# The weighing loops of an attention kernel turned: key tile outside, the four heads inside

## The chip, the cores and the metric

The kernel runs on one core of one Trainium2 chip. The metric is the device time of one execution in microseconds (us). A core has a matrix engine (TensorE, PE in the profile, its weight loads PEld), three engines for elementwise work (VectorE, DVE; ScalarE, ACT; GpSimd, POOL) and a queue engine (SyncE, SP) that here issues transfers. Each engine works its own instructions in order, and they meet through semaphores. PE takes a stationary operand (128 rows by up to 128 columns, put in by a weight load) and streams a moving operand through it; the products are added up in PSUM, a memory of 8 banks, each of 512 fp32 columns on 128 partitions. A matmul with the first-flag (`start=True`) overwrites what stands in its columns; one without it adds to them, or, where nothing was written in the bank since the last first-flag, writes them.

## The reference

Attention with grouped heads, then a gated block with a spatial mix. There are 8 batches, 16 query heads, 4 key/value heads (each serves four query heads), 384 positions and 64 columns a head.

```
scores = q @ k.T / sqrt(64)
attn   = exp(scores - max) ; attn = attn / (sum(attn) + 1e-9)
x      = attn @ v                       # heads side by side: [8, 384, 1024]
h      = relu(x @ w_in)                 # 1024 -> 1024
u, v   = h[..., :512], h[..., 512:]
v_n    = (v - mean(v)) / sqrt(var(v) + 1e-6)
v_s    = w_spatial @ v_n + b_spatial    # mixes the 384 positions
out    = (u * v_s) @ w_out              # 512 -> 1024
```

## The kernel before

One batch has 384 positions, so three tiles of 128 queries (`qt`) and three of 128 keys (`kt`, `NT` = 3). The 16 query heads go as two halves (`j`) of two key/value heads (`hh`), each with its group of four query heads (`G` = 4, index `i`). A set (`s`) is one query tile and one `j`: there are 6 sets a batch and 48 in all. For each set and each `hh` and `kt` the kernel makes one score matmul (L278, 64 rows of contraction, 512 columns: the 128 queries of four heads) into a bank, and ACT takes the exponent of it (L290) into the fp16 tile `aT`, which is laid out `[128 keys, kt, hh, 4 x 128 queries]`. The maximum isn't subtracted.

`weigh(b, s, hh)` (L292) multiplies these by the values. It takes a fresh bank `av` and issues twelve matmuls (L298): for each of the four heads `i` and each key tile `kt`, the stationary operand is the 128x128 block of `aT`, and the moving operand is a slice of `v1` with 65 columns. The slice holds the 64 value columns and one column of ones, so that the 65th column of the result is the sum of the exponents. Slices of `v1` lie next to each other in the order `[key/value head, kt]`, each `VW = D + 2` = 66 fp16 columns long (L46, L173); 65 of the 66 are read. Head `i` owns columns 65i to 65i+64 of the bank. In the kernel before, the loop over heads is outside and the loop over key tiles inside, so that the three matmuls of one head follow each other and add to the same columns. The first of each three has the first-flag. Behind the twelve, DVE takes the reciprocal of the four sums (L311) and multiplies (L313) into the fp16 tile `x16`. `weigh` is called 96 times, which makes 1152 matmuls and 1152 weight loads.

The rest follows on `x16`. It is transposed to `xt`: for the first batch by PE (L330) and a copy, for the others by a DMA that SP issues (`x_send`, L334, called behind the second `weigh` of every second set). Then come x @ w_in (`pv` L353 for the v half, `pu` L412 for the u half, with the relu on ACT, L423), the normalisation on DVE, ACT and POOL, the spatial mix (`psp` L431), the gate on POOL (L448) and x @ w_out (`po` L469). Queries and keys are transposed by PE at the beginning (L224 and L238, against an identity matrix that is the moving operand) and by DMA later.

The order of the work is written out by the program. A loop of 21 single units (L717) starts it: in each, two score matmuls, two exponents, then `weigh` where a set has ended. The steady loop (L738) takes one set a turn: six score matmuls, three exponents, some matmuls of the second block ("pour", which draws on the generator `gated`), the second `weigh` of the set before, more pouring, three exponents, pouring, the first `weigh` of this set, pouring. How much is poured follows the planner's costs in ns (`spend`, L85), and `weigh` is entered there with 372 ns. The `bank` function (L77) takes the bank that the planner expects to be free first. The change touches none of these numbers, so that the planner's order of all other instructions stays.

The lines of `weigh`, and of what calls it:

Of the kernel before, what the change touches and what calls it, by code (L numbers as in the profile page):

```python
# [17 lines left out]
def kernel(  # L18
# [21 lines left out]
    NT = S // P  # L40
    NK = DM // P
    NM = DH // P
    G = HQ // HKV
# [33 lines left out]
    def bank(shape, dtype, name):  # L77
        i = min(range(8), key=done.__getitem__)
        t = ps.tile(shape, dtype, name=name, tag=f"bank{i}")
        clock[nc.tensor] = max(clock[nc.tensor], done[i])  # L80
        done[i] = 1e12 + clock[nc.tensor]
        taken[name] = i
        return t

    def spend(ns):  # L85
        clock[nc.tensor] += ns

    def reads(eng, ns, name=None):
        clock[eng] = max(clock[eng], clock[nc.tensor] + 200.0) + ns
        if name:  # L90
            done[taken.pop(name)] = clock[eng]
# [200 lines left out]
    def weigh(b, s, hh):  # L292
        qt, j = divmod(s, 2)
        aT = aTs[b, s]
        av = bank([P, 512], FP32, f"av_{b}_{s}_{hh}")
        for i in range(G):
            for kt in range(NT):
                nc.tensor.matmul(  # L298
                    av[:, i * (D + 1) : (i + 1) * (D + 1)],
                    aT[:, kt, hh, i * P : (i + 1) * P],  # L300
                    v1[b % 2][:, 2 * j + hh, kt, 0 : D + 1],
                    start=(kt == 0),
                    stop=(kt == NT - 1),
                )
        if s == 0 and hh == 0:
            x16s[b] = att.tile([P, NT, DM], FP16, name=f"x16_{b}", tag="x16")
        o = av[:, 0 : G * (D + 1)].rearrange("p (i d) -> p i d", i=G)
        spend(372)
        r = small.tile([P, G, 1], FP32, name=f"r_{b}_{s}_{hh}", tag="r")
        reads(dve, 600.0, f"av_{b}_{s}_{hh}")  # L310
        dve.reciprocal(r, o[:, :, D : D + 1])  # L311
        c = j * 512 + hh * 256
        dve.tensor_tensor(  # L313
            x16s[b][:, qt, c : c + 256].rearrange("p (i d) -> p i d", i=G),
            o[:, :, 0:D],
            r.to_broadcast([P, G, D]),
            ALU.mult,
        )
        measure()
# [54 lines left out]
    def measure():  # L374
        while unmeasured:
            b, st = unmeasured.pop()
            reads(dve, 800.0)
            stats = small.tile([P, 6], FP32, name=f"stats_{b}_{st}", tag="stats")
            dve.bn_stats(stats, v_r[b, st])  # L379
            dve.bn_aggr(mvs[b][:, st], stats)  # L380
# [336 lines left out]
    for u in range(ALONE):  # L717
        for pair in units(u, 1):
            exp(*pair)
        spare = 736  # L720
        for f, args in todo.pop(u, []):
            f(*args)
            spare -= 224 if f in (q_turn, x_turn, k_turn) else 0
        for b, s in ends.pop(u, []):
            halves.setdefault(u, []).append((b, s, 0))
            halves.setdefault(u + (0 if s == 0 else 1), []).append((b, s, 1))
        for h in halves.pop(u, []):
            weigh(*h)
            spare -= 372
            if h[2]:  # L730
                turn_x(*h[:2], u)
        owed = pour(u, min(owed, 0) + spare)
    for u in sorted(halves):
        for h in halves[u]:
            weigh(*h)
    owed = 0.0
    late = [(b, s, hh) for u in (ALONE, ALONE + 1) for b, s in ends.pop(u, []) for hh in range(2)]
    for n in range(ALONE, total, NT):  # L738
        share = STEP * (0.85 if n < 90 else 1.0)
        exps = units(n, NT)  # L740
        for pair in exps[:NT]:
            exp(*pair)
        owed = pour(n, owed + share * F[0])
        for h in late:
            weigh(*h)
            if h[2]:
                turn_x(*h[:2], n)
        owed = pour(n, owed + share * F[1])
        for u in range(n, n + NT):
            for f, args in todo.pop(u, []):  # L750
                f(*args)
        for pair in exps[NT:]:
            exp(*pair)
        owed = pour(n, owed + share * F[2])
        late = []
        for u in range(n, n + NT):
            for b, s in ends.pop(u + 2, []):
                weigh(b, s, 0)
                late.append((b, s, 1))
        owed = pour(n, owed + share * F[3])  # L760
# [36 lines left out]
```

## Time and profile before

| what | value |
|---|---|
| median of three runs | 241.03 us (239.21, 241.6, 241.03) |
| the profiled execution, its own time | 239.56 us |
| its span in the profile | 237.5 us |
| instructions | 5921 |
| granted clock of PE | 1.0 of full speed |
| PE busy / ACT busy / DVE busy / POOL busy | 97% / 71% / 60% / 42% |
| transfers | 47.47 MB, mean 200 GB/s |

The span is the time between the first and the last instruction that the profiler saw on the core; 2.06 us of the execution lie around it. Busy shares are of the span. Matmuls are pipelined: a matmul's duration in the profile runs from its start to the end of its last write, and the next one starts well before that. What a matmul costs in a dense stream is therefore read from the distance of two starts.

### The profile page before, as it was taken

The page shows a single profiled execution, that of the slowest core. Times are in us where ns is not written, and L with a number is a line of the kernel's source. Part 1 is how long each engine was busy: PE and PEld are TensorE (multiplying, and loading weights), DVE is VectorE, ACT ScalarE, POOL GpSimd, SP SyncE. Part 2 cuts the span into 40 slices and gives each one's busy share as a digit, 9 for nine tenths or more (in the row PEclk, how much of TensorE's full clock was granted, in tenths as well). Part 3 has the DMA queues.
Part 4 walks back from the last instruction along what each step waited for, and adds up shares of the span by engine and source line. Part 5 has one row for each costly group of instructions (what it writes and reads, how often), then busy time and mean ns, then how long its engine had stood idle before and what let it go on. Part 6 is the DMA issues. An engine that isn't in the chain of part 4 may idle for free.

```text
span 237.5 us, 5921 instructions
## 1 busy us (share of the span) xinstructions
PE 231.4 (97%) x2312; PEld 124.3 (52%) x2312; DVE 142.8 (60%) x379; ACT 169.2 (71%) x348; POOL 100.9 (42%) x145
## 2 busy tenths in 40 slices
PE   7999999999999999999999999999999999999993
PEld 6555565645554545555464445555465455545541
DVE  2668774676447674566645577366744667367362
ACT  2899979969897869977697776986597776401211
POOL 3769663651465432275045800565022500360550
PEclk9999999999999999999999999999999999999999
DMA  6999959998999999997996599829912543240147
GB/s 199 286 328 308 280 107 194 228 224 223 292 220 258 322 296 176 365 199 176 171 323 200 168 199 300 266 88 158 260 21 44 114 147 95 48 177 0 66 201 266
DMA packets 67467, 47.47 MB, mean 200 GB/s; under 512 B 48336, under 2 KB 60416, under 8 KB 67440
## 3 DMA queue, kind: packets, MB, share of 16 engines
q1 hardware_dynamic: 62512, 39.86, 66.6%
q0 software_dynamic: 3952, 6.42, 11.9%
q10 hardware_dynamic: 976, 0.82, 1.2%
q8 instruction: 18, 0.29, 0.5%
q14 instruction: 9, 0.07, 0.1%
HBM read 25.95 MB, written 12.58 MB: 162 GB/s over the span
## 4 chain that ended last, share of the span: by engine, by line
PE 93%; DVE 3%; DMA 2%; ACT 1%; issue 0%; ACTq 0%
PE pu L412 18%; PE pv L353 18%; PE po L469 17%; PE sc L278 16%; PE av L298 15%; PE psp L431 7%; DMA q<-in_q_dram 2%; PE qps L238 1%; DVE x L313 1%; ACT aT L290 1%; DVE qT L216 1%; PE xps L330 1%; DVE osb L216 1%; PE kps L224 0%; DVE r L311 0%
## 5 line engine op out<-in xcount | busy, mean ns | idle before, releaser
L290 ACT ACTIVATE aT<-sc 128x512 f16<-128x512 f32 x288 | 147.4, 625 | 32.0 <-PE sc L278 31.4
L298 PEld LDWEIGHTS <-aT 128*128 128x128 f16 x1152 | 47.7, 97 | 17.0 <-issue 1.6
L298 PE MATMUL av<-v,aT 128*128 128x65 f16 x1152 | 51.6, 193 | 0.1
L353 PE MATMUL pv<-w_in,xt 128*128 128x512 f16 x192 | 50.8, 379 | 0.1
L469 PE MATMUL po<-w_out,gT 128*128 128x512 f16 (+2 forms) x196 | 50.5, 375 | 0.0
L412 PE MATMUL pu<-xt,w_in 128*128 128x384 f16 x256 | 49.9, 326 | 0.0
L397 POOL TENSOR_SCALAR vn<-vr,rstd,nmr 128x512 f16<-128x512 f32 x23 | 17.6, 779 | 71.3 <-DVE nmr L392 49.8
L448 POOL TENSOR_TENSOR gT<-vs,uT 128x384 f16<-128x384 f32 x31 | 32.4, 1058 | 32.4 <-DVE r L311 17.1
L313 DVE TENSOR_TENSOR x<-av,r 128x256 f16<-128x256 f32 x96 | 40.7, 424 | 3.3
L278 PE MATMUL sc<-qT,kT 64*128 64x512 f16 x288 | 42.2, 380 | 0.4 <-DVE qT L216 0.2
L311 DVE RECIPROCAL r<-av 128x4 f32<-128x4 f32 x96 | 17.1, 178 | 41.2 <-PE av L298 41.0
L216 DVE COPY osb<-po 128x512 f32<-128x512 f32 (+1 forms) x39 | 26.5, 682 | 17.3 <-PE po L469 17.3
L412 PEld LDWEIGHTS <-w_in 128*128 128x128 f16 x256 | 22.1, 97 | 17.1 <-issue 5.5
L423 ACT ACTIVATE uT<-pu 128x384 f16<-128x384 f32 x32 | 15.8, 493 | 16.3 <-PE pu L412 16.1
L469 PEld LDWEIGHTS <-gT 128*128 128x128 f16 x196 | 17.4, 97 | 17.4 <-issue 2.8
L353 PEld LDWEIGHTS <-xt 128*128 128x128 f16 x192 | 15.8, 97 | 17.9 <-issue 5.7
L278 PEld LDWEIGHTS <-kT 64*128 64x128 f16 x288 | 10.9, 94 | 25.0 <-issue 13.8
L431 PE MATMUL psp<-wsT,vn 128*128 128x384 f16 x96 | 22.2, 326 | 0.0
L443 DVE TENSOR_TENSOR vs<-psp,bias_bc 128x384 f32<-128x384 f32 x32 | 17.5, 551 | 7.0 <-PE psp L431 6.9
L367 DVE TENSOR_SCALAR vr<-pv 128x512 f32<-128x512 f32 x24 | 16.4, 682 | 8.5 <-PE pv L353 8.4
L201 POOL CAST q<-q 128x768 f16<-128x768 f32 x22 | 17.6, 831 | 7.5 <-DMA q<-in_q_dram 5.5
L379 DVE BATCH_NORM_STATS2 stats<-vr 128x6 f32<-128x512 f32 x24 | 16.4, 685 | 0.1
(47 smaller groups left out, 98.6 us busy)
## 6 DMA issues: line engine op xcount, KB each, us to landing
out_dram<-osb SPq DMA_DIRECT2D x21, 512.0 KB, 2.8
q<-in_q_dram SPq DMA_DIRECT2D x10, 768.0 KB, 7.4
v_None<-in_v_dram SPq DMA_DIRECT2D x6, 384.0 KB, 4.6
w_in<-in_moe_w_in_dram POOLq DMA_DIRECT2D x4, 512.0 KB, 10.3
k_None<-in_k_dram SPq DMA_DIRECT2D x5, 384.0 KB, 3.9
q<-in_q_dram POOLq DMA_DIRECT2D x2, 768.0 KB, 8.9
out_dram<-osb SPq DMA_DIRECT2D x5, 256.0 KB, 2.3
w_out<-in_moe_w_out_dram POOLq DMA_DIRECT2D x2, 512.0 KB, 6.8
```

The lines of the kernel that those rows point to most:

```text
L201: eng.tensor_copy(t16[:, :, :, hh, :], src[:, hh])
L216: (act.copy if eng is act else dve.tensor_copy)(o, i)
L278: nc.tensor.matmul(sc, kTs[b][rows, j, kt * P : (kt + 1) * P], qTs[b, j][rows, qt].rearrange("p (r i c) -> p i r c", r=G, i=G), start=True ...
L290: act.activation(a, sc, AF.Exp, scale=scale)
L298: nc.tensor.matmul(av[:, i * (D + 1) : (i + 1) * (D + 1)], aT[:, kt, hh, i * P : (i + 1) * P], v1[b % 2][:, 2 * j + hh, kt, 0 : D + 1], st ...
L313: dve.tensor_tensor(x16s[b][:, qt, c : c + 256].rearrange("p (i d) -> p i d", i=G), o[:, :, 0:D], r.to_broadcast([P, G, D]), ALU.mult,)
L353: nc.tensor.matmul(pv, xts[b][:, kt, st * P : (st + 1) * P], w_in16[:, kt, DH:DFF], start=(kt == 0), stop=(kt == NK - 1),)
L397: (dve if b == 0 and st == 1 else pool).tensor_scalar(vn, v_r.pop((b, st)), rstd[:, st : st + 1], nmr[:, st : st + 1], op0=ALU.mult, op1=A ...
L412: nc.tensor.matmul(pu[:, 0:S], w_in16[:, kt, m * P : (m + 1) * P], xts[b][:, kt, :], start=(kt == 0), stop=(kt == NK - 1),)
L431: nc.tensor.matmul(psp[:, 0:S], v_n[b, st][:, m * P : (m + 1) * P], wsT16[:, st, :], start=(st == 0), stop=(st == NT - 1),)
L448: pool.tensor_tensor(gT, vs, uT, ALU.mult)
L469: nc.tensor.matmul(po[:, 0:width], gTs[b][:, m, tt * P : (tt + 1) * P], w_out16[:, m, c0 : c0 + width], start=(m == 0), stop=(m == NM - 1),)
```

## The change

In `weigh` the two loops change places. The key tile is now outside, the four heads are inside. The same twelve products are formed, and each head's columns still receive key tiles 0, 1 and 2 in this order, so each sum is formed in the same order as before. What differs is that four matmuls in a row now read the same slice of `v1` and write four different stretches of the bank, and that a head's columns are added to by every fourth matmul. The first-flag is set on the first matmul of the bank alone; the first matmuls of heads 1 to 3 write columns in which nothing stands since that flag. The last-flag is on the twelfth matmul alone.

```diff
@@ -293,14 +293,14 @@
         qt, j = divmod(s, 2)
         aT = aTs[b, s]
         av = bank([P, 512], FP32, f"av_{b}_{s}_{hh}")
-        for i in range(G):
-            for kt in range(NT):
+        for kt in range(NT):
+            for i in range(G):
                 nc.tensor.matmul(
                     av[:, i * (D + 1) : (i + 1) * (D + 1)],
                     aT[:, kt, hh, i * P : (i + 1) * P],
                     v1[b % 2][:, 2 * j + hh, kt, 0 : D + 1],
-                    start=(kt == 0),
-                    stop=(kt == NT - 1),
+                    start=(kt == 0 and i == 0),
+                    stop=(kt == NT - 1 and i == G - 1),
                 )
```

## The prediction

> **What bounds the kernel now.** I read the busy times first, then the chain that ended last, then the stretches of time, then the group of the changed line, and last the start times of its matmuls.
>
> The page's busy times, its chain and three of its groups:
>
> ```profile
> PE 231.4 (97%) x2312; PEld 124.3 (52%) x2312; DVE 142.8 (60%) x379; ACT 169.2 (71%) x348; POOL 100.9 (42%) x145
> ...
> PE 93%; DVE 3%; DMA 2%; ACT 1%; issue 0%; ACTq 0%
> PE pu L412 18%; PE pv L353 18%; PE po L469 17%; PE sc L278 16%; PE av L298 15%; PE psp L431 7%; DMA q<-in_q_dram 2%; PE qps L238 1%; DVE x L313 1%; ACT aT L290 1%; DVE qT L216 1%; PE xps L330 1%; DVE osb L216 1%; PE kps L224 0%; DVE r L311 0%
> ...
> L298 PEld LDWEIGHTS <-aT 128*128 128x128 f16 x1152 | 47.7, 97 | 17.0 <-issue 1.6
> L298 PE MATMUL av<-v,aT 128*128 128x65 f16 x1152 | 51.6, 193 | 0.1
> ...
> L311 DVE RECIPROCAL r<-av 128x4 f32<-128x4 f32 x96 | 17.1, 178 | 41.2 <-PE av L298 41.0
> ```
>
> PE is on 93% of the chain, and the weighing matmuls (L298) hold 15% of it, 35.6 of 237.5 us: what is saved or lost in them reaches the end where no other engine sets the pace. The 193 ns are not what a matmul costs, since they overlap: 35.6 us over 1152 is 31 ns. DVE waits for av and not av for DVE.
>
> Stretches: columns are PE, weight loads, DVE, ACT, POOL, each busy us of the stretch, then clock, DMA share and GB/s.
>
> ```profile
> 12.00:30.00 18.00, 18.00 (x240) 9.76 (x239) 13.49 (x41) 17.44 (x36) 13.99 (x24) 1.00 1.13 307
> 30.00:60.00 30.00, 29.78 (x333) 16.31 (x331) 19.49 (x56) 24.56 (x51) 13.36 (x21) 1.00 0.99 196
> 60.00:100.00 40.00, 40.00 (x430) 21.33 (x425) 22.55 (x63) 34.47 (x73) 17.55 (x23) 1.00 1.09 272
> 100.00:150.00 50.00, 50.00 (x506) 25.83 (x505) 31.13 (x82) 38.71 (x81) 19.89 (x26) 1.00 0.91 225
> 150.00:203.00 53.00, 53.00 (x541) 28.10 (x538) 32.77 (x85) 40.36 (x83) 16.62 (x21) 1.00 0.52 123
> ```
>
> From 30 us on PE is full and ACT, the next, has 14 to 24% free. From 12 to 30 us ACT is busy 17.44 of 18: there it may set the pace with PE. The clock is 1.00 throughout, so no loop order can win or lose it.
>
> The timeline of two groups of 12 (start, length, what):
>
> ```profile
> 115.84 0.54 PE L298 MATMUL av<-v,aT 128*128 128x65 f16 x12
> 116.22 0.59 PE L353 MATMUL pv<-w_in,xt 128*128 128x512 f16 x2
> ...
> 118.48 0.53 PE L298 MATMUL av<-v,aT 128*128 128x65 f16 x12
> 118.85 0.33 PE L412 MATMUL pu<-xt,w_in 128*128 128x384 f16 x1
> ```
>
> Start to the start of what follows is 0.38 us in the first, 0.37 in the second. The trace holds single start times, and they say why. Mean ns from a matmul's start to the next one's, by key tile, over the 67 groups from 57 us to 200 us; the last column adds all twelve steps of a group. "v head" is 2j+hh; "at" is where its v slice starts, in bytes past a 16-byte boundary: slices are VW = 66 fp16 = 132 bytes apart (L46), so the start moves 4 bytes per slice (I take the tile to begin on a boundary).
>
> ```
> v head   kt 0 (at)   kt 1 (at)   kt 2 (at)   twelve
> 0        29.1 (0)    33.4 (4)    32.4 (8)    379
> 1        29.4 (12)   29.2 (0)    34.1 (4)    371
> 2        30.4 (8)    33.3 (12)   29.2 (0)    372
> 3        29.2 (4)    33.3 (8)    31.9 (12)   378
> ```
>
> A step is some 29.2 ns, and longer in exactly two sorts: key tile 1 and key tile 2, unless their slice starts on a 16-byte boundary. Key tile 0 never pays, wherever its slice starts. Twelve steps at 29.2 are 350.4 ns; the mean group takes 374.9. So 24.5 ns of a group are extra, over six paying steps on average (8, 4, 4, 8 by v head), 4.1 ns each. The first of a group pays 5.8 (head 0, 35.0) to 6.7 (head 1, 35.9), the later ones 3 to 4.
>
> **What the change removes, adds and moves.** Count: 96 groups of 12 matmuls, 12 weight loads each, before and after; no DMA, copy or activation is added, removed or moved past another. DVE's reciprocal and multiply stand behind the twelfth matmul as now. The order on every engine but PE stays, and x_send's place on SP's queue too.
>
> (1) *The steps.* Paying steps have three things in common: a slice that starts inside a 16-byte line, a slice that begins where the one before it ended (kt 1 after kt 0, kt 2 after kt 1; 130 bytes are read of 132), and an add to the columns written just before. A slice that starts inside a line and neither follows on the last nor adds (kt 0) is free. I take the second as the cause, together with the first: a matmul whose moving rows begin in the line in which the last one ended waits for it. An add to just-written columns alone doesn't do it: kt 1 of head 1 and kt 2 of head 2 add too, at 29.2. In the new order a slice is read four times, then the next: the step onto a following slice comes twice in a group, of which 2, 1, 1, 2 start inside a line, mean 1.5. Each stands alone, so I charge the price of a first one, 6 ns: 9 ns. Saved: 24.5 - 9 = 15.5 ns a group. The two ends: all extra goes, 24.5 ns; or each of the nine re-reads of a slice costs 6 too, 63 ns of extra, 38.5 lost. I take the re-reads at nothing: the nearest rows are the transposes, four matmuls that read one identity (L238), whose starts lie 56 ns apart for 128 columns, as little as any step of that size in the trace, and the jump back from kt 2 to kt 0, which is free.
>
> The Trainium skill (SBUF — State Buffer, Specifications) gives SBUF 16-byte lines and a penalty for each cross to a new one; that agrees with the 16 bytes of the table. By that rule alone a price belongs to a slice and not to its place in the order, and the change would save nothing; key tile 0 of heads 1 to 3, free at 12, 8 and 4 bytes, speaks against it.
>
> Of 96 groups 14 start before 30 us, where ACT is nearly full; I count them at nothing: 82 x 15.5 ns = 1.27 us (with them 1.49).
>
> (2) *The waits.* Weight loads of L298 carry 62 waits on ACT's semaphore: 12 on the first, 8 on the second, 42 on the third. They move to the first, fifth and ninth, so the last exp of a set gets six steps, 0.18 us, more. Three groups now stop at the step to kt 2, at 9.6, 54.4 and 202.8 us: 112, 305 and 86 ns, 0.41 us over normal steps. The first lies where ACT is full, and behind the second the score matmuls wait at 55.1 to 55.8 us for engines that are late anyway. I take 0.15 us, with 0 and 0.41 as ends. No wait is added; what stands behind a waiting load is PE's whole stream, as now.
>
> (3) *The flags.* One first-flag in place of four, 11 adding matmuls in place of 8. At 384 and 512 columns a matmul with the flag and those after it are one step (162 and 215 to 216 ns in pu and pv), so the flag has no price there; at 65 columns the trace can't part it from key tile 0. I take nothing; if it is the lack of the flag that makes a step pay, the ends are below.
>
> What is late next: from 60 us on nothing, PE stays full. Behind 203 us no weighing is left and the tail only moves up.
>
> **Sum.** 1.27 + 0.15 = 1.4 us off the profiled execution: 239.56 (span 237.5 and 2.06 around it) to 238.1. That execution is 0.6% under the median of the runs shown, 241.03; in proportion the median becomes 239.6, -0.6%. About 1% is what a measurement of this kernel can tell from no change: its three runs lie between 239.21 and 241.6.
>
> The Trainium skill (TensorE: Matmul & The Clock Gate, Back-to-back issue gap) gives columns/2.4 + 2.5 ns, 29.6 ns at 65: the free steps agree (29.2), the paying ones (31.9 to 34.1) don't. An estimate by that page of the Trainium skill is 355 ns a group in any order, which is 20 ns under the group as it is and some 1.7 us over the 82.
>
> **Rivals.**
> *All extra goes.* If what costs is the add to columns written one matmul before (with the line as a second condition), the new order, with four matmuls between adds, has none: 24.5 ns x 82 = 2.0 us, with all groups 2.35, and 0.15 to 0.41 of waits: 2.2 to 2.8 us, 237.4 to 236.8, on the median 238.8 to 238.2. For it: key tile 0 neither adds nor pays. Against: the two adding steps that are free.
> *Nothing comes of it.* If the step is set by the slice alone or by the weight load, the times stay: 239.56, on the median 241.0. For it: each weight load starts 1 to 3 ns after a matmul's start, in lockstep. Against: the price follows v head and not aT.
> *The flag pays.* If steps without first-flag pay when their slice starts inside a line, paying steps go from 8, 4, 4, 8 to 8, 7, 7, 11, 2.25 more a group at 4.1 ns: 0.9 us slower, 240.4, on the median 241.9.
> *Re-reading pays: slower.* If a slice whose first line was read one matmul before costs as an adjoining one does, nine re-reads and 1.5 crossings at 6 ns take the place of 24.5 ns: 38.5 x 96 = 3.7 us slower, 243.3, on the median 244.7 (+1.5%). It decides from (24.5 - 9)/9 = 1.7 ns a re-read on. For it: nothing at this length reads a slice twice in a row. Against: the identity's 56 ns.
>
> **How the numbers follow.** Forecast 0.42, all extra 0.27, nothing 0.13, flag 0.08, re-reading 0.10. A true -0.6% measures beyond -1% in a third of cases; all extra (-0.9 to -1.2%) in two thirds: faster 0.14 + 0.18 = 0.32, rounded up to 0.33. Slower: re-reading 0.09, half of flag 0.04, and 0.01: 0.14. Within 1%: 0.53. The range goes from all extra at its low end less run noise, 236.8, to the flag, 242.0, and leaves re-reading out.
>
> **What would show it.** Right: groups of 359 ns, steps of 29 ns within a key tile, some 35 at the fourth matmul of kt 0 and kt 1 or the one behind, none there where the next slice starts on a boundary. All steps at 29: the second rival. Steps of 33 in kt 0: the flag. Steps of 33 to 36 throughout: re-reading. Wrong it would also be if PE, once ahead, stood at the score matmuls waiting for ACT or DVE between 60 and 203 us.

## The result: 0.4% faster, by groups that are 10 ns shorter

The changed kernel takes 239.4 us (median of 20 runs, 238.4 to 242.18) against 240.14 us before (20 runs, 239.21 to 241.86). One run of the changed kernel, of 242.18 us, is a slow one and left out of the ratio. The ratio is 0.9964 with a 95% interval from 0.9946 to 0.9982: faster, by 0.2 to 0.5%. That is less than the 1% that three runs could have told from no change; it took twenty a side. The profiled execution takes 239.07 us and its span is 237.0 us, 0.5 less than before.

The page of the changed kernel, in the places that were read of the kernel before: busy times, the chain by engine and by line, the weighing matmuls and their loads, the reciprocal behind them.

```profile
PE 230.4 (97%) x2312; PEld 123.3 (52%) x2312; DVE 142.9 (60%) x379; ACT 169.4 (71%) x348; POOL 101.4 (43%) x145
...
PE 79%; DMA 15%; DVE 1%; POOL 1%; SPq 1%; issue 0%
PE pu L412 17%; PE po L469 16%; PE pv L353 15%; PE sc L278 12%; PE av L298 12%; PE psp L431 6%; DMA xt<-x 4%; DMA w_in<-in_moe_w_in_dram 4%; DMA q<-in_q_dram 3%; DMA v_None<-in_v_dram 2%; DMA qT<-q 2%; POOL vn L397 1%; PE qps L238 1%; DVE osb L216 1%; POOL q L204 0%; SPq L256 0%
...
L298 PEld LDWEIGHTS <-aT 128*128 128x128 f16 x1152 | 47.0, 97 | 16.8 <-issue 2.0
...
L298 PE MATMUL av<-v,aT 128*128 128x65 f16 x1152 | 50.5, 193 | 0.0
...
L311 DVE RECIPROCAL r<-av 128x4 f32<-128x4 f32 x96 | 17.1, 178 | 40.8 <-PE av L298 40.5
```

PE's busy time falls by 1.0 us and that of the weighing matmuls by 1.1 (51.6 to 50.5); every other engine stays within 0.5. That the chain now has 15% DMA where it had 2% doesn't mean that PE has become idle; it is as full as before. A chain takes the latest releaser at each step, and a small shift is enough to lead it over a transfer. One of these transfers does count, though, the transposed x on which PE waits at 85 us (below). In the chain it is this piece:

```profile
75.15 10.13 DMA xt<-x
```

Stretches of the changed kernel: PE, weight loads, DVE, ACT, POOL, each busy us, then clock, DMA share, GB/s.

```profile
30.00:60.00 30.00, 29.79 (x336) 16.38 (x334) 19.61 (x56) 24.67 (x51) 14.46 (x23) 1.00 1.04 198
60.00:100.00 40.00, 39.93 (x431) 21.20 (x426) 22.57 (x63) 34.46 (x73) 17.73 (x23) 1.00 1.09 272
100.00:150.00 50.00, 50.00 (x513) 25.88 (x512) 31.07 (x82) 38.89 (x82) 20.10 (x27) 1.00 0.94 229
150.00:203.00 53.00, 53.00 (x542) 28.08 (x539) 32.82 (x86) 40.49 (x85) 16.45 (x20) 1.00 0.52 121
```

Into the stretch from 100 to 150 us fall 513 matmuls where 506 did, into that from 150 to 203 us 542 where 541 did. The two groups shown of the kernel before, now:

```profile
115.75 0.53 PE L298 MATMUL av<-v,aT 128*128 128x65 f16 x12
116.11 0.59 PE L353 MATMUL pv<-w_in,xt 128*128 128x512 f16 x2
...
118.38 0.53 PE L298 MATMUL av<-v,aT 128*128 128x65 f16 x12
118.75 0.65 PE L412 MATMUL pu<-xt,w_in 128*128 128x384 f16 x3
```

Start to next start is 0.36 us (0.38 before) and 0.37 us (0.37 before too, at this rounding). The single start times, over the same 67 groups (57 to 200 us), give 364.8 ns for twelve steps, 10.05 less than the 374.9 of before. The mean steps in issue order, for v head 0 before and for all four v heads after, are

```
before, head 0  29.2 35.0 32.4 29.2 32.6 32.6 29.1 32.9 32.4 29.1 32.9 32.0   379
after,  head 0  29.2 35.0 29.1 29.2 33.5 29.4 29.2 29.2 34.2 29.2 29.1 29.4   366
after,  head 1  29.2 34.1 29.2 29.1 29.2 29.2 35.0 29.2 32.5 29.2 29.2 29.2   364
after,  head 2  29.2 33.4 29.1 29.1 33.5 29.1 29.3 29.7 29.1 34.6 29.1 29.2   364
after,  head 3  29.1 32.2 29.2 29.2 34.1 29.2 29.1 29.1 34.3 29.1 29.2 31.1   365
```

Eight dear steps of head 0 have become three. The slice changes between the fourth and the fifth matmul and between the eighth and the ninth. Six of the eight new slices begin inside a line, and behind each of these the first matmul has a dear step: the fifth and the ninth in heads 0 and 3, the ninth in head 1, the fifth in head 2. The two that begin on a line's start have none (29.2 at the fifth of head 1, 29.1 at the ninth of head 2). But every head also has a dear second step, and heads 1 and 2 one more at the seventh and the tenth (head 3 a smaller one at the twelfth), where no slice changes.

**Where 10 ns a group went.** Start times of the same matmul in both profiled executions, compared:

| from the first matmul of | us | all of PE | weighing alone |
|---|---|---|---|
| the stream to group 14 | 1.0 to 30.5 | +0.10 us | +0.04 us |
| group 14 to 28 | 30.5 to 58.1 | -0.08 | -0.17 |
| group 28 to 95 | 58.1 to 202.8 | -0.43 | -0.67 |
| group 95 to the end | 202.8 to 233.5 | -0.06 | -0.07 |

The 0.67 us are 67 times 10.05 ns. Of these 0.24 are given back: 0.12 by a single step behind a score matmul at 84.9 us, 0.12 by the matmuls of the four other lines; a matmul that follows a group takes 0.4 to 1.3 ns more than before, by line. The step at 84.9 us is a wait for a transfer: the `pv` matmul that comes next is the first to read a new transposed x. The weight load that waits for it, first before the change and then after:

```profile
85.29 0.11 PEld L353 LDWEIGHTS <-xt 128*128 128x128 f16 x2 [0.45 <-DMA xt<-x]
```

```profile
85.32 0.11 PEld L353 LDWEIGHTS <-xt 128*128 128x128 f16 x2 [0.56 <-DMA xt<-x]
```

The transfer landed at 85.25 us before and at 85.28 after. PE came to this place 0.09 us earlier than before and left it 0.03 us later, so that nothing won up to there is left, and all that the span is shorter was won behind it. In the first 30 us nothing is gained at all. A lead of 0.11 us at 15.5 us ends at a transfer of w_in. The timeline there, before and after:

```profile
16.08 0.38 PE L353 MATMUL pv<-w_in,xt 128*128 128x512 f16 x1
```

```profile
15.48 0.52 PE L298 MATMUL av<-v,aT 128*128 128x65 f16 x12
16.24 0.38 PE L353 MATMUL pv<-w_in,xt 128*128 128x512 f16 x1 [0.23 <-DMA w_in<-in_moe_w_in_dram]
```

The group is followed by a matmul that reads w_in at 16.24 us, where in the kernel before it stood at 16.08: the transfer landed at 16.20 us in this execution and at 16.03 in the one before, and PE waited for it in both.

### The profile page after: what moved, and what is told of

Same layout as the page of the kernel before. It is cut to its first block, busy times and chain, and to the rows that moved or that the text cites. A ratio compares the mean times of both kernels' runs of the same rounds, so it can differ in the third digit from the quotient of the medians.

```text
span 237.0 us, 5921 instructions
## 1 busy us (share of the span) xinstructions
PE 230.4 (97%) x2312; PEld 123.3 (52%) x2312; DVE 142.9 (60%) x379; ACT 169.4 (71%) x348; POOL 101.4 (43%) x145
## 4 chain that ended last, share of the span: by engine, by line
PE 79%; DMA 15%; DVE 1%; POOL 1%; SPq 1%; issue 0%
PE pu L412 17%; PE po L469 16%; PE pv L353 15%; PE sc L278 12%; PE av L298 12%; PE psp L431 6%; DMA xt<-x 4%; DMA w_in<-in_moe_w_in_dram 4%; DMA q<-in_q_dram 3%; DMA v_None<-in_v_dram 2%; DMA qT<-q 2%; POOL vn L397 1%; PE qps L238 1%; DVE osb L216 1%; POOL q L204 0%; SPq L256 0%
## 5 line engine op out<-in xcount | busy, mean ns | idle before, releaser
L290 ACT ACTIVATE aT<-sc 128x512 f16<-128x512 f32 x288 | 147.7, 618 | 31.5 <-PE sc L278 30.5
L298 PEld LDWEIGHTS <-aT 128*128 128x128 f16 x1152 | 47.0, 97 | 16.8 <-issue 2.0
L353 PE MATMUL pv<-w_in,xt 128*128 128x512 f16 x192 | 50.9, 380 | 0.4 <-DMA w_in<-in_moe_w_in_dram 0.2
L298 PE MATMUL av<-v,aT 128*128 128x65 f16 x1152 | 50.5, 193 | 0.0
L469 PE MATMUL po<-w_out,gT 128*128 128x512 f16 (+2 forms) x196 | 50.5, 375 | 0.0
```

The source lines that it names most:

```text
L290: act.activation(a, sc, AF.Exp, scale=scale)
L298: nc.tensor.matmul(av[:, i * (D + 1) : (i + 1) * (D + 1)], aT[:, kt, hh, i * P : (i + 1) * P], v1[b % 2][:, 2 * j + hh, kt, 0 : D + 1], st ...
L353: nc.tensor.matmul(pv, xts[b][:, kt, st * P : (st + 1) * P], w_in16[:, kt, DH:DFF], start=(kt == 0), stop=(kt == NK - 1),)
L469: nc.tensor.matmul(po[:, 0:width], gTs[b][:, m, tt * P : (tt + 1) * P], w_out16[:, m, c0 : c0 + width], start=(m == 0), stop=(m == NM - 1),)
```

## The experiments

After the result there were three theories on the cause and two on the rest. **Line theory** (the forecast's): a matmul whose moving slice begins in the 16-byte line where the last one ended costs some ns. **Column theory** (all extra goes): an add to columns written one matmul before costs. **Flag theory**: a matmul without first-flag costs. For the 14.4 ns over twelve times 29.2 that the change leaves there were the **rate** and the **weight theory**, told below. All are read from groups, since most are worth less than one run's noise: "group" is the mean of twelve steps over the groups from 57 to 200 us, with waits over 60 ns left out. A time without a number of runs is that of a single run; beside it stands a single run of the kernel before, 240.26 us for the first four and 240.23 us for the next four, and a median of 240.56 us over 23 runs for the last four. Single runs of the kernel before spread from 239.2 to 241.9 us, so a single time proves little.

One wait above all differs from run to run by more than the groups do, the one for the transposed x at 85 us. From the last score matmul to the `pv` matmul behind it there are 0.31 us where PE doesn't wait, 0.33 in the kernel before and 0.45 in the changed one; in the runs below it is between 0.31 and 1.79 us. It doesn't follow the length of the groups: two runs with 375 ns a group have 0.31 and 1.57.

### Slices as before, columns as after

```diff
-        for kt in range(NT):
-            for i in range(G):
+        for n in range(G * NT):
+            for i, kt in ((n % G, n % NT),):
...
-                    start=(kt == 0),
-                    stop=(kt == NT - 1),
+                    start=(n == 0),
+                    stop=(n == G * NT - 1),
```

> The twelve matmuls of a group go diagonally: head n mod 4, key tile n mod 3. So the value slices follow each other as in the kernel before (kt 0, 1, 2, 0, ...), while every matmul writes other columns than the one before it, as in the changed kernel; the first-flag is on the first matmul alone. Twelve steps take 375 ns before and 365 ns after (mean of the groups from 57 to 200 us). Line theory (a slice that begins in the 16-byte line where the last one ended costs): 375 ns, with the dear steps at kt 1 and kt 2 that are off a line's start. Column theory (adding to columns written one matmul before costs): 365 ns or less. Whole time: 239.6 by the first, 239.1 by the second.

Measured: 374.9 ns a group, and head by head the steps of before: 379.3, 370.5, 371.7, 378.0 against 379.4, 370.6, 371.7, 377.9. The whole takes 240.03 us. Its timeline, at the same two groups:

```profile
116.28 0.54 PE L298 MATMUL av<-v,aT 128*128 128x65 f16 x12
116.66 0.59 PE L353 MATMUL pv<-w_in,xt 128*128 128x512 f16 x2
...
118.93 0.53 PE L298 MATMUL av<-v,aT 128*128 128x65 f16 x12
119.30 0.33 PE L412 MATMUL pu<-xt,w_in 128*128 128x384 f16 x1
```

0.38 and 0.37 us, as before the change. Each matmul writes other columns than the one before it, as in the changed kernel, and nothing is won: the column theory falls. Adding to what the matmul before has just written costs nothing that the groups show.

### Columns as before, slices the other way round

```diff
         for i in range(G):
-            for kt in range(NT):
+            for kt in reversed(range(NT)):
...
-                    start=(kt == 0),
-                    stop=(kt == NT - 1),
+                    start=(kt == NT - 1),
+                    stop=(kt == 0),
```

> Heads outside and key tiles inside as before, but the key tiles in the order 2, 1, 0. A head's three matmuls still add to the same columns one after the other, but no slice begins where the last one ended: each begins 132 bytes before the last, or 264 bytes on. Line theory: the steps at adjoining slices lose their price, 365 ns a group as after the change. Column theory: 375 ns as before. Whole time: 239.1 by the first, 239.6 by the second.

Measured: 364.7 ns a group, the changed kernel's length, with the loops of before. The whole takes 240.16 us, not the 239.1 expected. Beside the profiled execution of the kernel before, two waits have taken the gain in this run: 0.73 us more at 50.9 us (PE waits for the cast of the values on POOL) and 0.37 at 85.7 us (for the transposed x). The timeline shows what the groups do:

```profile
116.76 0.53 PE L298 MATMUL av<-v,aT 128*128 128x65 f16 x12
117.13 0.59 PE L353 MATMUL pv<-w_in,xt 128*128 128x512 f16 x2
```

0.37 us where the ascending order has 0.38. So the direction in which the slices follow each other counts.

### The flags alone

```diff
-                    start=(kt == 0),
-                    stop=(kt == NT - 1),
+                    start=(kt == 0 and i == 0),
+                    stop=(kt == NT - 1 and i == G - 1),
```

(in the kernel before, loops untouched)

> The kernel before with nothing but the flags of the change: the first-flag on the first matmul of the bank alone, the last-flag on the twelfth alone; the loops stand as before. Flag theory (a matmul without first-flag whose slice starts inside a line costs): the steps at key tile 0 of heads 1 to 3 rise from 29.2 to 33 ns, 384 ns a group, 240.4 us. Line and column theories: 375 ns, steps as before, 239.6 us.

Measured: 374.75 ns a group, key tile 0 at 29.2 to 30.2 ns as before. The flags have no price. The whole takes 240.89 us; 1.24 us of it are the wait for the transposed x, which is 1.57 us from start to start here:

```profile
84.61 0.82 PE L278 MATMUL sc<-qT,kT 64*128 64x512 f16 x6
86.62 0.60 PE L353 MATMUL pv<-w_in,xt 128*128 128x512 f16 x2 [1.19 <-DMA xt<-x]
```

The transfer landed at 86.58 us, where it landed at 85.25 in the kernel before, so this time says nothing on the flags.

### One slice for all

```diff
-                    v1[b % 2][:, 2 * j + hh, kt, 0 : D + 1],
+                    v1[b % 2][:, 2 * j + hh, 0, 0 : D + 1],
```

> The kernel before, heads outside, key tiles inside, flags as before, but all matmuls of a group read the value slice of key tile 0: the values of key tiles 1 and 2 are left out of the result. Columns are added to one matmul after the other, as before; the moving rows are the same all through a group. Line theory: 365 ns a group as after the change, 239.1 us. Column theory: 375 ns, 239.6 us. If a group takes less than the 365 of the changed kernel, its two steps onto a next slice have a price of their own.

Measured: 363.75 ns a group, 239.19 us. With no change of slice at all a group is 1.1 ns shorter than the changed kernel's: two changes of slice cost about that much together. The other 13.4 ns over 350.4 come without any change of slice, and they differ by its start: 367.8 ns at 0 bytes past a line (head 0), 359.6 at 4 (head 3), 362.7 at 8 (head 2), 364.9 at 12 (head 1). Dear steps come at the second matmul and then every fourth or fifth, though every matmul reads the same bytes. That looks like something that runs short a little each time and is paid now and then.

This run also gives the price of a shared line. Each v head's three slices have starts whose groups it measures; what the kernel before takes above their mean is 16.0, 6.5, 6.7 and 15.3 ns for v heads 0 to 3, which have 8, 4, 4 and 8 steps onto a slice in a shared line. That is 1.6 to 2.0 ns a step in every head. The changed kernel, with 2, 1, 1 and 2 such steps, is 2.1, 0.1, -0.7 and 2.7 ns above, the descending order -0.5, 3.1, 1.2 and 0.

### Every slice on a line's start, in both orders

```diff
-    VW = D + 2
+    VW = D + 8
```

Once in the kernel before, once in the changed one: slices lie 144 bytes apart, nine whole lines.

> The kernel before with value slices 72 fp16 columns apart in place of 66 (144 bytes, nine 16-byte lines; 65 columns are read as before). Every slice starts on a line, and none shares a line with the next. Line theory: the loops as before, but no dear step at kt 1 and kt 2; what stays is what a slice at 0 bytes has when it is read twelve times (head 0 of the run with one slice), 368 ns a group against 375, and the pattern is the same for all four heads. If only the adjoining in time counts (kt 1 after kt 0) and not the shared line: 375 ns.

> The changed kernel with value slices 72 columns apart, all on a line's start. Line theory: loop order no longer matters, 368 ns a group as in the run with the old order and this spacing, 3 ns more than the changed kernel at spacing 66.

Measured: 367.45 ns a group in the old order and 367.4 in the new, all four heads between 367.2 and 367.7; 239.85 and 238.79 us. Where no two slices share a line, the order of the loops makes no difference to the group. That the two times differ by 1 us comes from elsewhere: in the old order PE waits 0.93 us longer for the transposed x at 85 us (1.24 us from start to start, 0.31 in the new order). The line theory stands; the 368 expected were read off head 0 of the run with one slice, so that nothing but the start is left of the price.

### 64 columns: what the rest is

The rest has two candidates. A slice of 65 columns takes nine lines, that is 72 places for 65 columns. What a column takes is in the trace: 512 columns have steps of 215.5 ns and 384 of 162, so 0.418 ns a column. Nine lines at that pace are 30.1 ns, a little over the step of 29.2: what is short would add up and be paid now and then (rate theory). Or weight loads of 128 columns come no faster than one in 30.4 ns (weight theory).

```diff
-                    av[:, i * (D + 1) : (i + 1) * (D + 1)],
+                    av[:, i * (D + 1) : i * (D + 1) + D],
...
-                    v1[b % 2][:, 2 * j + hh, kt, 0 : D + 1],
+                    v1[b % 2][:, 2 * j + hh, kt, 0:D],
...
-        dve.reciprocal(r, o[:, :, D : D + 1])
+        dve.reciprocal(r, o[:, :, 0:1])
```

(in the changed kernel; in the first of the two also `VW = D` and no ones)

> The changed kernel with 64 value columns in place of 65 and slices 64 columns apart: the column of ones is left out, and the reciprocal is taken of the first value column, so the result is not normalised. Each slice is 128 bytes, eight whole lines. What is left after the change (a dear step of 4 to 6 ns some three times a group) has two theories. Rate theory: a slice of 65 columns takes nine lines, 72 places, where the step takes 29.2 ns, and the lines come at 2.4 columns a ns, 30 ns a slice; what is short adds up and is paid now and then. With eight lines, 26.7 ns, nothing is short: all steps 28.8 ns, 345 ns a group. Weight theory: weight loads of 128 columns come no faster than one in 30.4 ns: dear steps stay, 364 ns a group.

> The same 64 columns, ones left out and no normalisation, but slices 66 columns apart as in the changed kernel, so that they start at 0, 4, 8 or 12 bytes past a line: eight lines at 0, nine elsewhere. Rate theory: steps of 28.8 ns without dear ones for a slice at 0, dear ones for the others, mean 30.2: 357 ns for heads 0 to 2, 362 for head 3. Weight theory: 364 ns as with eight lines.

Measured on whole lines: 353.3 ns a group and no dear step left, for head 0: 28.1 29.2 30.1 29.1 29.9 29.3 30.0 29.3 30.0 29.0 30.0 29.1. Off the line: 358.4, by head 359.4, 356.7, 355.8 and 361.8, where 357, 357, 357 and 362 were expected, and steps of 32 to 34 are back. The rate theory comes within 2.4 ns of each head here. An odd start and a ninth line go together in this pair; but 65 columns that begin on a line's start (the run before this) fill nine lines too and have dear steps (367.4), so an odd start isn't needed for them. The theory was wrong on the floor, 345: steps go up and down between 29 and 30, mean 29.4 in place of 28.8. And it gives 361 ns for 65 columns wherever they start, where 360 to 368 were measured. It is the better supported of the two, not shown.

### 32 columns: can weight loads come faster?

```diff
-                    av[:, i * (D + 1) : (i + 1) * (D + 1)],
+                    av[:, i * (D + 1) : i * (D + 1) + 32],
...
-                    v1[b % 2][:, 2 * j + hh, kt, 0 : D + 1],
+                    v1[b % 2][:, 2 * j + hh, kt, 0:32],
```

(in the changed kernel, with `VW = D` and no ones, so on whole lines; the reciprocal is taken of the first column, and the multiply on DVE reads the 32 columns twice)

> The changed kernel with 32 value columns in place of 65 and slices 64 columns apart, on a line's start: the ones and half of the values are left out, the result holds the first 32 twice and is not normalised. With 64 columns on whole lines no dear step was left, but the steps stayed at 29 and 30 in turn, 353 ns a group and not 345. If the columns set the step (32 in place of 64 at 2.4 a ns), it falls to some 16 to 25 ns, 190 to 300 ns a group. If something beside the columns, the weight load of 128 columns being the nearest, comes no faster than one in 29.4 ns, the group stays at 353 ns.

Measured: 303.8 ns a group, a little over the 190 to 300 expected, every step but the first at 25.0 to 25.3 ns; 236.42 us. Weight loads of 128 columns can follow each other at 25 ns, so their own pace is not what holds 64 or 65 columns at 29 and more; the weight theory falls. What holds 64 columns at 29.4 ns where columns alone, by 0.418 ns each, would take 27 stays open. That the step sinks to 25.0 and not lower agrees with the Trainium skill (TensorE: Matmul & The Clock Gate, Wait — 56ns, not 53.3ns?), which gives about 25 ns as the least start-to-start time of small matmuls. The group in the timeline:

```profile
115.68 0.46 PE L296 MATMUL av<-v,aT 128*128 128x32 f16 x12
115.99 0.59 PE L351 MATMUL pv<-w_in,xt 128*128 128x512 f16 x2
```

0.31 us where the changed kernel has 0.36 (lines are two up, since the ones are left out).

### The best start for a slice, in both orders

```diff
-    VW = D + 2
+    VW = D + 8
...
-        pool.memset(v1[i][:, :, :, D:VW], 1.0)
+        pool.memset(v1[i][:, :, :, D + 2:VW], 1.0)
...
-            v1[b % 2][:, g0:g1, :, 0:D].rearrange("p g t d -> p (g t) d"),
+            v1[b % 2][:, g0:g1, :, 2 : D + 2].rearrange("p g t d -> p (g t) d"),
...
-                    v1[b % 2][:, 2 * j + hh, kt, 0 : D + 1],
+                    v1[b % 2][:, 2 * j + hh, kt, 2 : D + 3],
```

> The changed kernel with value slices 72 columns apart that start two columns in, 4 bytes past a line's start; no slice shares a line with the next. In the run with one slice, head 3, whose slice starts at 4 bytes, had the shortest groups, 360 ns. Line and rate theory: 360 ns for all four heads, dear steps of 3 ns every fourth matmul, 15 ns a group under the kernel before and 5 under the changed one: 1.4 us off the kernel before, ratio 0.994. If the place of the start doesn't matter: 365 to 367 ns, ratio 0.996.

> The kernel before, loops and flags as they were, with value slices 72 columns apart that start 4 bytes past a line's start. Line theory: the loop order is worth nothing once no two slices share a line: 360 ns a group and ratio 0.994, as with the loops turned. If the turned loops do anything beside parting the shared lines, this group is longer than that of the kernel with the same spacing and the turned loops.

Measured with the loops turned: 359.9 ns a group, for head 0 29.0 32.3 29.3 29.4 three times over, a mean step of 30.0 ns, close to the 30.1 estimated for nine lines. 238.83 us (12 runs) against 240.56 (23 runs), ratio 0.9951, interval 0.9926 to 0.9976. With the loops as before: 359.9 ns too, 239.71 us (12 runs), ratio 0.996, interval 0.9927 to 0.9993. The timelines, first of the turned loops, then of the old ones:

```profile
115.66 0.52 PE L298 MATMUL av<-v,aT 128*128 128x65 f16 x12
116.02 0.59 PE L353 MATMUL pv<-w_in,xt 128*128 128x512 f16 x2
```

```profile
117.58 0.52 PE L298 MATMUL av<-v,aT 128*128 128x65 f16 x12
117.94 0.59 PE L353 MATMUL pv<-w_in,xt 128*128 128x512 f16 x2
```

0.36 us both. By the groups, a spacing and a start, without any turning of loops, do what the change does and 5 ns a group more. By time neither can be told from the changed kernel, whose interval overlaps both; over 96 groups the 5 ns are 0.5 us.

### A start at 2 bytes

The same with one column in place of two ahead of the slice.

> The changed kernel with slices 72 columns apart that start one column in, 2 bytes past a line's start. With one slice the groups took 360, 363, 365 ns at 4, 8, 12 bytes and 368 at 0. If the price grows with the columns of the first line that aren't used: 358 ns at 2 bytes. If it is the last line with a single used column (at 0 bytes) that costs: 360 ns or less, too. If it falls from 0 to 4 in even steps: 364 ns.

Measured: 368.4 ns a group (239.01 us), as long as at 0 bytes. Of the three expectations none is met: the price neither grows with the unused columns of the first line nor falls in even steps. The Trainium skill (SBUF — State Buffer, Specifications) asks for at least two hits in each line for full bandwidth. At 0 bytes the last line has one column and at 2 bytes two, with the same length: that condition doesn't explain it. At 4, 8 and 12 bytes the groups take 360, 363 and 365 ns. Why 4 is the best start is open.

## Why the prediction was right, and where its terms were off

**What bounds the kernel.** Right in the main: PE is full in both, and the weighing's gain shows in the start times of what follows, but only from 85 us on. There PE waits for the transposed x, which the prediction didn't have, and what was won before is lost.

**Step (1), the cause.** Right, and shown: the order of the slices is what counts (diagonal and descending order), neither the columns nor the flags, and the price goes when no two slices share a line (both orders at a spacing of 72 columns, with slices on a line's start and 4 bytes past it).

**Step (1), the size.** 15.5 ns a group were forecast, 10.05 came. Two terms were mis-sized. The whole extra of 24.5 ns was put down to shared lines. The runs part it: some 11 ns are shared lines (374.9 less the 363.75 of one slice), and 13.4 are what slices of 65 columns cost in any order, by their start. So a step onto a slice in a shared line was charged 4.1 to 6 ns and costs some 1.9. After the change these steps were charged 9 ns a group and cost 1.1. The two errors stand against each other, and that they did is luck: it is why the sum was nearer than its parts. The table of before held two hints. In heads 1 and 2 four dear steps cost 20 to 21 ns in all, 5 each, in heads 0 and 3 eight cost 27 to 29, 3.5 each; a price per shared line alone would have been the same everywhere. And key tile 0 of head 2, counted as free, stands at 30.4 ns, 1.2 over the floor.

**Where the dear steps lie.** Half right. They were to come at the fourth matmul of key tiles 0 and 1 or the one behind, and not where the next slice starts on a boundary. The one behind has them in all six cases, and the two boundary cases have none. Not foreseen were the second step of every group and one more in heads 1 to 3. These don't need a change of slice: the run with one slice has such steps too, at the second matmul and every fourth or fifth from there.

**Re-reading at nothing, flags at nothing.** Right. Where no two slices share a line, the order that never reads a slice twice in a row and the one that does so nine times take the same: 367.45 and 367.4 ns, and 359.9 both at the other start. The flags alone leave 374.75.

**The first 14 groups at nothing.** Right in size (0.04 us lost), though the place that shows at 16 us is not ACT but a transfer of w_in.

**Step (2), the waits.** 0.15 us were taken. At 9.6 and 202.8 us the waits inside the groups are gone, at 54.4 us one of 305 ns has become a step of 125, and the matmul behind that group stands 287 ns in place of 124: that one only moved. The stretch from 30.5 to 58.1 us gains 0.08 us, where 14 groups of 10 ns would give 0.14 without any wait. What is left is some 0.05 us at 202.8 us.

**The sum.** 1.4 us against 0.5 us between the two profiled executions (239.56 to 239.07), and 0.6% against 0.36%, interval 0.18 to 0.54%. Two things made the difference. The term of step (1), 82 x 15.5 ns = 1.27 us, was too large: it measured 82 x 10.05 = 0.82. And some of that was given back, 0.24 us between 58 and 203 us and 0.09 between 30 and 58; before that, 0.10 us were lost to waits at the beginning. Nothing had been set aside for this: "from 60 us on nothing, PE stays full" missed the transposed x at 85 us, which takes 0.12 us, and the matmuls behind a group, which grew by 0.4 to 1.3 ns.

That the forecast median, 239.6 us, lies 0.2 from the measured 239.4 is luck as well. It was counted from a median of 241.03 over three runs, and twenty runs put the kernel before at 240.14; 0.6% off that would be 238.7. The measured gain lies between the forecast and no gain at all, so the time alone would not have told the forecast from the rival that nothing comes of it. The groups do: 364.8 ns, against 374.9 for no effect, 359 forecast and 350 if all extra went. One small slip: 20 ns a group over 82 groups are 1.6 us and not 1.7.

## What to carry to other kernels

Where short matmuls bound the kernel, read single start times, by the operands' addresses, before turning loops: the pattern of 29 and 33 ns named the cause, and the group's mean hid it. Give short moving slices their own 16-byte lines, and try the start within the line: here that is worth 15 ns a group where the order of the loops is worth 10, and makes the order free, though the times of the two can't be told apart. A price that is read off as "per event" should be tested against cases with fewer events: here half the events cost seven tenths, and a second cause was in it. And where PE is full, ask which transfers have only just landed when it gets to them: a gain ahead of such a place is lost there.

## What the runs showed of the hardware

- Matmuls of 65 columns that add to columns written one matmul before cost no more than others (374.9 ns a group in both), and first-flags cost nothing (374.75 with one, 374.9 with four).
- A moving slice that begins in the 16-byte line where the last one ended costs 1.6 to 2.0 ns, 11 ns a group here; in descending order about 1 ns a group is left (364.7 against 363.75 with one slice). That the line has 16 bytes is read off the kernel before: steps onto slices that start 4, 8 and 12 bytes past a multiple of 16 (counted from the tile's start) are dear, those onto a multiple of 16 aren't.
- 65 columns of two bytes run at 30.0 ns a matmul at best (start 4 bytes past a line) and at 30.6 to 30.7 ns at 0 and 2 bytes; 64 columns on whole lines at 29.4, off them at 29.9; 32 columns at 25.0, but for a group's first step, with a weight load each. Why the start matters is open.
